# Two early flushes of postponed instructions, and keys moved before queries, in the routed-attention stage of a fused kernel

## The chip, the cores and the metric

The kernel runs on one core of one Trainium2 chip. The core has TensorE (PE; its weight loads are shown as PEld), VectorE (DVE), ScalarE (ACT), GpSimd (POOL) and SyncE (SP, which here only issues DMAs). The metric is device time in microseconds. Three timed runs of the kernel before took 784.69, 784.79 and 788.32 us, median 784.79.

## The reference

Three layers follow each other; all numbers are float32.

```
# 1: attention over pooled queries: B=4, H=8, S=1152, D=64
q_pool = q.reshape(B, H, 576, 2, D).mean(axis=3)
attn = softmax(q_pool @ k.T / 8);  y = attn @ v          -> x [4, 576, 512]
# 2: four causal attention experts; each token uses its best two
logits = x @ w_gate;  w = softmax over the two largest
for e in range(4):
    a = softmax(causal(x @ wq[e] @ (x @ wk[e]).T / 8))
    out += where(e chosen) * w * (a @ (x @ wv[e]) @ wo[e])
# 3: gated layer: causal convolution of 5 taps over the sequence
gate = sigmoid(conv(out));  result = (gate * (out @ w_val)) @ w_out
```

## The kernel before

Every engine's program is in the order in which the Python code calls the instructions; waits between engines are put in by the framework. Most float32 operands of a matmul are split in a high and a low half, and a product is the sum of three (high·high, low·high, high·low). So what TensorE makes in PSUM is evacuated twice: ScalarE writes the high half, VectorE the low one, which is the PSUM value less the high half (`split2`, L224 and L225).

The change lies in the second layer (stage 2, about 513 to 712 us of the span). For each batch b of four, experts go in two pairs g, and each pair has five query tiles in the order 1, 3, 2, 4, 0 (`ORDER`). That makes 40 steps n, ten for a batch: n = 10 to 14 are the first pair of b = 1, n = 20 to 24 that of b = 2. So n = 12 and n = 22 are the third tile (tile 2) of the first pair.

In step n the loop does the following, in this order: the normalisation factors of tile n - 1 (`norm2`, VectorE, then a multiplication on GpSimd, L786), the scores of tile n (`scores2`, L750 or L757 on TensorE; then maximum with the mask L759 and row minimum L760 on VectorE), one piece of filling work, the transposes of tile n - 2 (`transp2`, L822 or L810, evacuated in turn by ScalarE and VectorE, L798 and L800), the exponential of tile n (`expo2`, L771 or L773), and then more filling work up to a budget.

The filling work is the list `fill`. Its pieces are the projections of a pair (`proj`: for queries, w = 0, and keys, w = 1, two halves of 12 matmuls each, L242), the value projections (`vgate`, L275), the value products (`av2`, L837 and L850, which give y of a pair) and the output mix (`mix`, eight halves of six matmuls, L869, evacuated by L870 and L871). The mix of batch b - 1 is put on `fill` when y of its second pair is done; that falls in steps 12, 13 and 14 of the ten.

What a piece leaves for later goes on the list `late2`: the low half that VectorE makes (L225), the moves of a finished key or query tile (`move`: DMAs on SyncE from `hl` to the tiles that the scores read, four for keys, L256, and six for queries, L258 to L261), the four loads of a later batch's x (`load2`, L196), and, for `av2`, the function that puts the mix on `fill`. `late2` is emptied when the next piece has been issued (`pop`), or by `flush()`, which stands at the end of step 0 and of each tenth step, and at the start of a step when `fill` is empty. The conv taps of the mixed output (L215, VectorE) are `rides`: one or a few are issued behind a piece or at the end of a step.

PSUM for all the filling work is a pool of four buffers (`ps_m`); the tiles `hl` come from a pool of two.

Of the kernel before, what the change touches and what calls it, by code (L numbers as in the profile page):

```python
# [20 lines left out]
def tile_kernel(ctx, tc, q, k, v, w_gate, wq, wk, wv, wo, w_val, conv_w, w_out, wo_t, out):  # L21
# [42 lines left out]
    def f(ap):  # L64
        return ap.bitcast(F32)
# [127 lines left out]
    def load2(b):  # L193
        xh = xh_p.tile([P, KT, 2, SQ], F32R, name="xh")
        for t in range(KT):
            nc.sync.dma_start(f(xh[:, t]), f(x_d[b][:, t]))  # L196
        return [[xh[:, t, i] for i in range(2)] for t in range(KT)]
# [23 lines left out]
    late2, urgent, rides = [], [], []  # L221

    def split2(hi, lo, src, mul=1.0):
        act.activation(hi, src, AF.Copy, scale=mul)  # L224
        late2.append(lambda: dve.scalar_tensor_tensor(out=lo, in0=src, scalar=mul, in1=f(hi), op0=ALU.mult, op1=ALU.subtract))  # L225
# [3 lines left out]
    def proj(xh, g, then=None):  # L229

        box = {}

        def half(w, hf):
            if hf == 0:
                box[w] = hl2.tile([P, 2, SQ], F32R, name="hl")
            hl = box[w]
            cs = slice(w * ED + g * P, w * ED + (g + 1) * P)
            qsl = slice(hf * HQ, (hf + 1) * HQ)
            ps = ps_m.tile([P, 512], F32, name="a")
            ops = [(wi, xi, t) for t in range(KT) for wi, xi in THREE]  # L240
            for o, (wi, xi, t) in enumerate(ops):
                pe.matmul(ps[:, 0:HQ], lhsT=wqk[wi][:, t, cs], rhs=xh[t][xi][:, qsl], start=o == 0, stop=o == len(ops) - 1)  # L242
            split2(hl[:, 0, qsl], hl[:, 1, qsl], ps[:, 0:HQ], -scale if w == 0 else 1.0)
            if hf == 1:
                if w == 1 and then:
                    late2.append(then)
                late2.append(lambda: move(w))

        def move(w):
            hl = box[w]  # L250
            for r in range(2):
                rs = slice(64 * r, 64 * r + 64)
                for i in range(2):
                    src = hl[64 * i:64 * i + 64]
                    if w == 1:
                        nc.sync.dma_start(f(ks[g][i][rs]), f(src))  # L256
                    elif i == 0:
                        nc.sync.dma_start(f(qs[g][0][rs, 0:SQ]), f(src[:, r]))  # L258
                    else:
                        nc.sync.dma_start(f(qs[g][1][rs, 0:4 * P]), f(src[:, r, 0:4 * P]))  # L260
                        nc.sync.dma_start(f(qs[g][1][rs, SQ:]), f(src[:, r, 4 * P:]))  # L261

        return [(1.48, lambda w=w, hf=hf: half(w, hf)) for w in range(2) for hf in range(2)]

    def vgate(xh):
        v2 = v_p.tile([P, 5, ED + E], F32, name="v2")
# [442 lines left out]
    def value(yhs, b, m, hf, then):  # L709

        qsl = slice(hf * HQ, (hf + 1) * HQ)
        ps = ps_m.tile([P, 512], F32, name="a")
        ops = [(wi, yi, g) for g in range(EP) for wi, yi in THREE]
        for o, (wi, yi, g) in enumerate(ops):
            pe.matmul(ps[:, 0:HQ], lhsT=wf[:, g, wi, m * P:(m + 1) * P], rhs=yhs[b, g][:, yi, qsl], start=o == 0, stop=o == len(ops) - 1)  # L715
        late2.append(lambda: then(ps[:, 0:HQ], m, qsl))
# [16 lines left out]
    with ExitStack() as s2l:  # L733
# [61 lines left out]
        def evac(dst, src):  # L795
            turn[0] += 1
            if turn[0] % 2:
                act.activation(dst, src, AF.Copy)  # L798
            else:
                dve.tensor_copy(dst, src)  # L800
# [92 lines left out]
        def ahead(n):  # L893
            return (WORK[steps[n][2]][0] if n < len(steps) else 0) + (WORK[steps[n - LAG][2]][1] if LAG <= n < len(steps) + LAG else 0)
# [28 lines left out]
        def flush():  # L923
            now, late2[:] = late2[:], []
            for a in now:
                a()

        assert not fill and not late2 and not urgent
        for n in range(len(steps) + LAG):
            if n < len(steps):  # L930
                b, g, i = s = steps[n]
                if n % 5 == 0:
                    pts[b, g] = (pt_p2.tile([P, 4, 2, SQ], F32, name="pt"), pt_p2.tile([R64, 2, R64], F32, name="pt4"))
                    if g == 0 and b:
                        fill += proj(xh[b], 1, (lambda: xh.update({3: load2(3)})) if b == 2 else None)
                        if b == B - 1:
                            fill.append((0, lambda: late2.append(begin3)))
                    if n == 10 * B - 5:
                        buf = [f(c2.tile([P, 2, SQ], F32R, name=f"k20{i}")) for i in range(2)]
                        bufs = [c2.tile([P, SQ + R64], F32R, name=f"q20{i}") for i in range(2)]  # L940
                        v2 = v_p.tile([P, 5, ED + E], F32, name="v2").rearrange("p t c -> p (t c)")
                        first3["raw"] = [[buf[t // 2][:, t % 2] for t in range(KT)], [f(bufs[t])[:, 0:SQ] if t < 2 else v2[:, (t - 2) * SQ:(t - 1) * SQ] for t in range(KT)]]
                        raws = [(0.74, lambda i=i, m=m, hf=hf: value(yhs, i, m, hf, lambda ps, m, qsl: evac(first3["raw"][i][m][:, qsl], ps))) for i in range(2) for m in range(KT) for hf in range(2)]
                        fill += raws[0:14]
                    if b == 0 and g == 1:
                        buf = y0_p.tile([P, EP, 2, SQ], F32R, name="y0")
                        yhs.update({(0, i): buf[:, i] for i in range(EP)})
                    if b == 1 and g == 0:
                        buf = y12_p.tile([P, 2, EP, 2, SQ], F32R, name="y12")
                        yhs.update({(1 + j, i): buf[:, j, i] for j in range(2) for i in range(EP)})  # L950
                if n % 10 == 5 and b + 1 < B:
                    fill += proj(xh[b + 1], 0)
                if n % 10 == VG and b + 1 < B:
                    v2s[b + 1], gws[b + 1], vg = vgate(xh[b + 1])
                    fill += vg
                if n == 0:
                    fill += proj(xh[0], 1)
                if n == FD:
                    fill += [(2.6, lambda g=g: fold(g)) for g in range(EP)]
            t = 0.0  # L960
            left = 5 - n % 5
            own = [ahead(m) for m in range(n, n + left)]
            budget = max(FL, (sum(c for c, _ in fill) + (PEND if 10 <= n and n % 10 < PN else 0) + sum(own)) / left) - own[0]

            room = [3]

            def ride():
                if urgent:
                    urgent.pop(0)()
                    return  # L970
                if rides and room[0]:
                    room[0] -= 1
                    rides.pop(0)()

            def pop(rider=True):
                c, a = fill.pop(0)
                now, late2[:] = late2[:], []
                a()
                for x in now:
                    x()  # L980
                if rider:
                    ride()
                return c

            if 0 <= n - 1 < len(steps):
                norm2(steps[n - 1], gws[steps[n - 1][0]])
            if n < len(steps):
                scores2(s)
            if fill:
                t += pop(RD[n % 5])  # L990
            else:
                flush()
            if n >= LAG:
                b1, g1, i1 = steps[n - LAG]
                transp2(steps[n - LAG], pts[b1, g1])
                if i1 == ORDER[-1]:
                    if g1 == 1:
                        then = (lambda b1=b1: fill.extend(mix(b1, [yhs[b1, 0], yhs[b1, 1]]))) if b1 < B - 1 else begin_last
                    else:
                        then = (lambda: None) if b1 < B - 1 else load_wo3  # L1000
                    fill[IN:IN] = av2(v2s[b1], pts[b1, g1], g1, yhs[b1, g1], then)
            if n < len(steps):
                expo2(s)
            if n == 0:
                flush()
            while fill and t < budget:
                t += pop()
            ride()
            if n == 9:
                xh[2] = load2(2)  # L1010
            if n % 10 == 9:
                flush()
                while urgent:
                    urgent.pop(0)()
# [118 lines left out]
```

## Time and profile before

| | |
|---|---|
| timed runs, median | 784.79 us |
| profiled execution, its own time | 786.26 us |
| its span in the trace | 784.5 us |
| TensorE busy | 758.7 us (97%) |
| VectorE busy | 570.9 us (73%) |
| ScalarE busy | 448.4 us (57%) |
| GpSimd busy | 306.4 us (39%) |
| mean granted clock of TensorE | 0.998 |

The profiled execution is another one than the timed runs, and 1.47 us above their median. The span is what the trace holds; 1.76 us of the execution's time lie around it. The rows below name a line of the kernel, an engine, and what is written from what ("hl<-a" is the tile hl written from PSUM tile a). A figure in brackets is the time that the engine stood idle before the row, with what ended it.

### The profile page before, as it was taken

Reading aid. Unit: us, or ns where it says so; the run is one execution under the profiler, and the core shown is the slowest. Engines: PE = TensorE matmul, PEld = TensorE weight load, DVE = VectorE, ACT = ScalarE, POOL = GpSimd, SP = SyncE. Lnnn points to the kernel's source line nnn. Section 1 sums busy time; section 2 is a strip of 40 time slices with the busy share of each in tenths; the row PEclk is TensorE's granted clock in tenths of the full one; section 3 lists DMA queues with packets and bytes.
Section 4 is the critical chain, followed back from the end, with each engine's and each line's share of the span. In section 5 each row is a group of like instructions: output and inputs, shape, how many; then the busy total and the mean of one; then the engine's idle time right before and its main releaser. Section 6 shows DMA issues by size and latency. Waiting matters only on the chain.

```text
span 784.5 us, 14786 instructions
## 1 busy us (share of the span) xinstructions
PE 758.7 (97%) x5332; PEld 623.6 (79%) x5332; DVE 570.9 (73%) x1063; ACT 448.4 (57%) x988; POOL 306.4 (39%) x412
## 2 busy tenths in 40 slices
PE   6999999999999999999999999999989889989998
PEld 4777877878778778778778778898989779877887
DVE  5777888898988888567657756257679779887730
ACT  5665566566466566656656665344454554648532
POOL 4565575674765764652542501023222312230000
PEclk9999999999999999999999999999999999999999
DMA  7787868868878788667657581484524743900112
GB/s 237 179 204 221 242 185 228 243 181 236 208 238 241 204 239 257 178 184 209 155 162 229 135 293 43 92 239 102 162 67 123 199 99 92 302 8 14 73 63 94
DMA packets 86825, 134.51 MB, mean 171 GB/s; under 512 B 21600, under 2 KB 58976, under 8 KB 86752
## 3 DMA queue, kind: packets, MB, share of 16 engines
q1 hardware_dynamic: 86752, 133.57, 60.4%
q8 instruction: 42, 0.69, 0.4%
q14 instruction: 31, 0.25, 0.1%
HBM read 53.37 MB, written 21.76 MB: 96 GB/s over the span
## 4 chain that ended last, share of the span: by engine, by line
PE 84%; DVE 7%; DMA 3%; ACT 2%; SPq 1%; issue 1%; POOLq 0%; DVEq 0%; ACTq 0%
PE s L416 21%; PE t L464 19%; PE t L494 18%; PE o L1049 6%; PE a L242 5%; PE a L275 4%; DMA k<-hl 3%; PE a L850 2%; PE s L750 2%; PE a L715 2%; PE a L822 1%; DVE nm L760 1%; PE t L453 1%; PE a L869 1%; DVE gp L215 1%
## 5 line engine op out<-in xcount | busy, mean ns | idle before, releaser
L421 DVE TENSOR_REDUCE nm<-s 128x1 f32<-128x1152 f32 x144 | 195.5, 1358 | 37.0 <-PE s L416 30.9
L427 ACT ACTIVATE p<-s,nm 128x1152 f32<-128x1152 f32 x144 | 175.9, 1222 | 37.1 <-DVE nm L421 28.3
L464 PE MATMUL t<-ident,p 128*128 128x128 f32 x1296 | 194.1, 280 | 2.5 <-DVE pt L474 1.9
L472 ACT ACTIVATE pt<-t 128x384 f32<-128x384 f32 x224 | 99.9, 489 | 145.7 <-PE t L464 136.6
L464 PEld LDWEIGHTS t<-ident,p 128*128 128x128 f32 x1296 | 147.4, 141 | 41.1 <-ACT pt L472 17.0
L494 PE MATMUL t<-pt,vn 128*64 128x320 f32 (+1 forms) x1152 | 146.8, 409 | 0.0
L416 PE MATMUL s<-ka,qst 128*128 128x384 f32 x480 | 127.5, 369 | 6.8 <-ACT ka L545 6.8
L494 PEld LDWEIGHTS t<-pt,vn 128*64 128x64 f32 x1152 | 80.0, 137 | 55.8 <-issue 5.3
L416 PE MATMUL s<-kb,qst 128*128 128x384 f32 x480 | 121.1, 361 | 1.0 <-ACT p L427 0.9
L474 DVE COPY pt<-t 128x384 f32<-128x384 f32 x208 | 107.4, 548 | 13.1 <-PE t L464 9.6
L786 POOL TENSOR_TENSOR p<-p,sm 128x512 f32<-128x512 f32 (+3 forms) x32 | 40.1, 1253 | 122.1 <-DVE sm L784 96.3
L416 PEld LDWEIGHTS s<-kb,qst 128*128 128x128 f32 x480 | 79.8, 191 | 8.3 <-issue 6.2
L416 PEld LDWEIGHTS s<-ka,qst 128*128 128x128 f32 x480 | 78.1, 193 | 8.1 <-ACT ka L545 7.2
L442 POOL COPY rm<-rs 128x256 f32<-128x256 f32 x31 | 12.4, 399 | 130.1 <-PE t L464 73.3
L496 DVE TENSOR_TENSOR xf<-t,rb 128x256 f32<-128x256 f32 (+1 forms) x32 | 14.6, 458 | 63.1 <-PE t L494 62.3
L371 POOL TENSOR_TENSOR hlk<-kt,hlk 128x384 fp32r<-128x384 f32 x45 | 45.3, 1006 | 1.0
L771 ACT ACTIVATE p<-s,nm 128x256 f32<-128x256 f32 (+3 forms) x64 | 33.1, 525 | 19.4 <-DVE nm L760 19.4
L242 PE MATMUL a<-xh,wqk 128*128 128x288 f32 x288 | 42.7, 299 | 0.0
L503 POOL CAST xt<-xf 128x256 fp32r<-128x256 f32 (+1 forms) x32 | 13.6, 424 | 71.8 <-DVE xf L496 71.7
L215 DVE SCALAR_TENSOR_TENSOR gp<-x,cw,gp 128x572 f32<-128x572 f32 (+3 forms) x48 | 39.5, 825 | 0.5
L242 PEld LDWEIGHTS a<-xh,wqk 128*128 128x128 f32 x288 | 39.4, 188 | 0.4
L760 DVE TENSOR_REDUCE nm<-s 128x2 f32<-128x512 f32 (+4 forms) x40 | 32.4, 811 | 1.4
(176 smaller groups left out, 1095.5 us busy)
## 6 DMA issues: line engine op xcount, KB each, us to landing
ka<-hlk SPq DMA_DIRECT2D x90, 192.0 KB, 3.2
kb<-hlk SPq DMA_DIRECT2D x90, 192.0 KB, 3.6
vn<-in_v_dram SPq DMA_DIRECT2D x16, 576.0 KB, 7.6
k<-hl SPq DMA_DIRECT2D x32, 288.0 KB, 4.9
qt<-in_q_dram SPq DMA_DIRECT2D x15, 576.0 KB, 5.4
kt<-in_k_dram SPq DMA_DIRECT2D x15, 576.0 KB, 6.3
xh<-x_d SPq DMA_DIRECT2D x12, 576.0 KB, 6.5
x_d<-xt SPq DMA_DIRECT2D x16, 320.0 KB, 4.1
```

Source lines behind the costliest of these rows:

```text
L215: dve.scalar_tensor_tensor(out=gp[:, n:], in0=x[:, 0:SQ - n], scalar=cw[:, m, c:c + 1], in1=gp[:, n:], op0=ALU.mult, op1=ALU.add)
L242: pe.matmul(ps[:, 0:HQ], lhsT=wqk[wi][:, t, cs], rhs=xh[t][xi][:, qsl], start=o == 0, stop=o == len(ops) - 1)
L371: late.append(lambda: pool.tensor_tensor(out=hlk[:, 1, gs], in0=kt[:, gs], in1=f(hlk[:, 0, gs]), op=ALU.subtract))
L416: pe.matmul(ps[:, 0:GW], lhsT=a, rhs=c, start=o == 0, stop=o == len(ops) - 1)
L421: dve.tensor_reduce(d["nm"], d["s"][:, :, 0:GW], axis=AX.XY, op=ALU.min)
L427: act.activation(d["p"], d["s"][:, :, 0:GW], AF.Exp, bias=d["nm"], scale=-1.0, accum_out=sums[(2 * n + u) % len(sums)][:, i:i + 1])
L464: pe.transpose(ps[:, j * P:(j + 1) * P], p[:, g, j * P:(j + 1) * P], ident)
L472: act.activation(dst, src, AF.Copy)
L474: dve.tensor_copy(dst, src)
L494: pe.matmul(ps[64 * h:64 * h + 64, 0:N], lhsT=vn[:, h, j, :], rhs=pt[:, j, h, :], start=j == 0, stop=j == C - 1)
L760: dve.tensor_reduce(nm, ps[:, :, 0:w], axis=AX.X, op=ALU.min)
L1049: pe.matmul(ps[:, 0:w], lhsT=hl[xi][:, kt, t * P - a:(t + 1) * P - a], rhs=end3["wo3"][:, kt, wi, c:c + w], start=o == 0, stop=o == len(op ...
```

## The change

Two edits. At the end of steps 12 and 22 `flush()` is called. In `proj` the keys (w = 1) are projected and moved first, then the queries (w = 0); the loads of the next x (`then`, in batch 2 alone), which stood ahead of the key moves at the end of the projections, stand behind the query moves.

```
-                if w == 1 and then:
+                late2.append(lambda: move(w))
+                if w == 0 and then:
                     late2.append(then)
-                late2.append(lambda: move(w))
...
-        return [(1.48, lambda w=w, hf=hf: half(w, hf)) for w in range(2) for hf in range(2)]
+        return [(1.48, lambda w=w, hf=hf: half(w, hf)) for w in (1, 0) for hf in range(2)]
...
             if n == 9:
                 xh[2] = load2(2)
+            if n in (12, 22):
+                flush()
             if n % 10 == 9:
                 flush()
```

VectorE at the end of step 12 and the start of step 13; `y_6724` is y of the batch, `sm` the normalisation factors, `s` the scores and `nm` their minimum:

```order
 L225 SCALAR_TENSOR_TENSOR hl<-a,hl 128x288
-L780 TENSOR_SCALAR sm<-sm 128x2
-L781 RECIPROCAL sm<-sm 128x2
-L784 TENSOR_TENSOR sm<-sm,gw 128x2
-L759 TENSOR_TENSOR s<-s,cmask_78 128x64
-L760 TENSOR_REDUCE nm<-s 128x2
-L762 TENSOR_TENSOR nm<-nm 128x1
 L225 SCALAR_TENSOR_TENSOR y_6724<-a,y_6724 128x128
 L225 SCALAR_TENSOR_TENSOR y_6724<-a,y_6724 128x448
+L780 TENSOR_SCALAR sm<-sm 128x2
+L781 RECIPROCAL sm<-sm 128x2
+L784 TENSOR_TENSOR sm<-sm,gw 128x2
```

The two low halves of y now stand ahead of the factors of step 12 and the maximum and minima of step 13, which follow in the same order as before. Further on in steps 13 and 14, three conv taps stand behind the copy of the first transposes and ahead of the factors of the next tile, where none stood.

TensorE in step 13, from the second half of its scores on; `a<-y,wos` is the mix, `a<-ident,p` a transpose:

```order
 L757 MATMUL s<-k_6218,q_6214 128x288 x2
 L757 MATMUL s<-k_6219,q_6215 128x288 x2
+L869 MATMUL a<-y_6724,wos_95 128x288
+L869 MATMUL a<-y_6724,wos_96 128x288
+L869 MATMUL a<-y_6724,wos_95 128x288 x2
+L869 MATMUL a<-y_6724,wos_96 128x288
+L869 MATMUL a<-y_6724,wos_95 128x288
 L822 MATMUL a<-ident,p 128x128 x8
 L869 MATMUL a<-y_6724,wos_95 128x288
```

The first half of the mix moves ahead of the eight transposes. Four halves now stand ahead of the scores of step 14, where two stood; four follow them instead of six.

SyncE at the end of the projections of batch 2 (steps 20 to 22); `k_6220`, `k_6221`, `q_6216` and `q_6217` are the key and query tiles of the second pair, `xh` is x of batch 3, `g_d` the stored convolution. Before:

```order
L258 DMA q_6216<-hl 64x576
L260 DMA q_6217<-hl 64x512
L261 DMA q_6217<-hl 64x64
L880 DMA g_d_71<-gp 128x576
L196 DMA xh<-x_d_70 128x1152 x4
L256 DMA k_6220<-hl 64x1152
L256 DMA k_6221<-hl 64x1152
L256 DMA k_6220<-hl 64x1152
L256 DMA k_6221<-hl 64x1152
```

And now:

```order
L256 DMA k_6220<-hl 64x1152
L256 DMA k_6221<-hl 64x1152
L256 DMA k_6220<-hl 64x1152
L256 DMA k_6221<-hl 64x1152
L258 DMA q_6216<-hl 64x576
L260 DMA q_6217<-hl 64x512
L261 DMA q_6217<-hl 64x64
L258 DMA q_6216<-hl 64x576
L260 DMA q_6217<-hl 64x512
L261 DMA q_6217<-hl 64x64
L196 DMA xh<-x_d_70 128x1152 x4
```

The four key moves go from behind the loads to the front, and the loads stand behind all ten moves.

## Rows read from the trace of the kernel before

**Rows 1.** Waits of TensorE, 490 to 712 us: total, times, longest

```profile
PE a L869 <- DVE y L225: 2.6, 2, 1.3
PE s L750 <- issue: 1.7, 1, 1.7
PE a L869 <- ACT pt L798: 1.4, 2, 0.7
PE s L750 <- DMA k<-hl: 0.7, 2, 0.5
```

**Rows 2.** Timeline of TensorE, third batch, then second: start, us, instructions, idle before

```profile
614.25 0.44 PE L837 MATMUL a<-pt,v 128*64 128x128 f32 x4 [0.55 <-DVE pt L800]
618.80 1.04 PE L822 MATMUL a<-ident,p 128*128 128x128 f32 x8
631.53 0.47 PE L750 MATMUL s<-k,q 128*128 128x256 f32 x2 [1.70 <-issue]
632.58 1.76 PE L242 MATMUL a<-xh,wqk 128*128 128x288 f32 x12
...
564.22 0.44 PE L837 MATMUL a<-pt,v 128*64 128x128 f32 x4
581.67 1.76 PE L242 MATMUL a<-xh,wqk 128*128 128x288 f32 x12
```

**Rows 3.** Stretches after the mix waits, second and third batch: busy, PEclk, DMA, GB/s

```profile
572.00:578.00 6.00, 5.26 (x29) 5.26 (x30) 4.29 (x12) 3.66 (x10) 1.15 (x1) 0.72 0.20 40
620.00:626.00 6.00, 4.16 (x31) 3.92 (x32) 5.32 (x16) 3.66 (x10) 2.61 (x2) 1.00 1.03 342
```

**Rows 4.** Timeline of ScalarE and VectorE, steps 22 and 23

```profile
617.37 0.55 ACT L224 ACTIVATE y<-a 128x448 fp32r<-128x448 f32 x1 [1.85 <-PE a L850]
619.77 0.17 DVE L780 TENSOR_SCALAR sm<-sm 128x2 f32<-128x2 f32 x1 [2.35 <-ACT p L771]
621.91 0.81 DVE L225 SCALAR_TENSOR_TENSOR y<-a,y 128x128 fp32r<-128x128 f32 x2
```

**Rows 5.** Timeline, the operations of the chain in front of step 25

```profile
621.30 0.68 DVE L762 TENSOR_TENSOR nm<-nm 128x1 f32<-128x1 f32 x1
622.08 0.74 ACT L773 ACTIVATE p<-s,nm 128x576 f32<-128x576 f32 x1 [1.60 <-DVE nm L762]
625.93 0.55 DVE L800 COPY pt<-a 128x384 f32<-128x384 f32 x1
626.39 1.66 DVE L215 SCALAR_TENSOR_TENSOR gp<-x,cw,gp 128x573 f32<-128x573 f32 x2
626.98 0.44 ACT L870 ACTIVATE x<-a 128x288 f32<-128x288 f32 x1
627.27 0.54 ACT L871 ACTIVATE gp<-a,cw 128x288 f32<-128x288 f32 x1
...
601.08 0.15 DVE L780 TENSOR_SCALAR sm<-sm 128x1 f32<-128x1 f32 x1
602.28 0.42 DVE L760 TENSOR_REDUCE nm<-s 128x2 f32<-128x256 f32 x1
```

**Rows 6.** Timeline, a tap beside a GpSimd multiplication

```profile
642.39 1.89 POOL L786 TENSOR_TENSOR p<-p,sm 128x1024 f32<-128x1024 f32 x1 [4.12 <-DVE sm L784]
643.84 1.06 DVE L215 SCALAR_TENSOR_TENSOR gp<-x,cw,gp 128x575 f32<-128x575 f32 x1
```

**Rows 7.** SyncE's queue in step 22, and landing times, 600 to 640

```profile
616.38 2.07 SPq L196 DMA_DIRECT2D xh<-x_d  x4
618.54 2.67 SPq L256 DMA_DIRECT2D k<-hl  x4
...
k<-hl SPq DMA_DIRECT2D x4, 288.0 KB, 11.3
...
DMA to landing us min/median/max: 4.7/6.5/10.5
```

**Rows 8.** Stretch of steps 15 to 19: busy time of each engine

```profile
582.00:610.00 28.00, 28.00 (x218) 25.89 (x217) 25.76 (x65) 13.02 (x41) 6.16 (x5) 1.00 0.38 96
```

## The prediction

> **What bounds the kernel now.** I read the page's busy shares first: TensorE works for 97% of the span, so only time in which TensorE stands still, or runs slowly, can be won. The change touches the second stage alone, so the next view is the list of waits of TensorE in that stage [rows 1]. Four of its rows matter. Twice the output mix (L869) waits for the low half of y that VectorE makes (2.6 us together), twice just before that for ScalarE's copy out of PSUM (1.4), once the scores (L750) wait 1.7 us with no releaser named, and twice they wait for the key move (0.7 together, the longer 0.5). The timeline of TensorE gives the places [rows 2]. In the third batch (b = 2, step 22 and on) the value products (L837) start at 614.25. The mix waits fall in step 23 and the 1.70 in front of step 25, and the first projection of step 25 (L242) starts at 632.58: 18.33 us for this piece. The same piece of the second batch goes from 564.22 to 581.67, 17.45 us. Its TensorE work is the same, and it has the mix waits (2.0) but not the wait for keys (1.7 and 0.2). So by its waits the second batch should take 18.33 - 1.9 = 16.4. The missing 1.05 us is the clock: the granted clock is 0.72 of full over 572 to 578, so the lower of its two levels, 1.2 GHz, held for part of it after these waits, and 1.00 over 620 to 626 after the same waits of the third batch [rows 3].
>
> **The change part by part.**
>
> *The flush at the end of steps 12 and 22.* What it releases is the two low halves of y and the eight halves of the mix. Now VectorE makes y low at 621.91, behind the sums, maximum and minimum of the next tile, though ScalarE had y high at 617.92 and VectorE stood idle for 2.35 us until 619.77 [rows 4]. By the new order y low stands ahead of that group, so its 0.81 us falls into the idle time and is over by 618.8, when TensorE finishes the scores of step 23. The first half of the mix now stands there in the order, ahead of the eight transposes, and its PSUM buffer is not the one that the copy of those transposes frees. So both mix waits go, 2.0 us in each batch.
>
> *What is late next.* The piece of the third batch holds 18.33 - 2.0 - 1.7 - 0.2 = 14.4 us of TensorE work, so the projection of step 25 could start at 614.25 + 14.4 = 628.65. By the new order it must wait for a VectorE copy (L800, of the transposes of step 24), and ahead of that copy stand, since the mix comes out earlier, four conv taps instead of one. I follow VectorE from the end of L762 at 621.98, which nothing earlier moves [rows 5]. ScalarE then does the exponential of step 23 (0.74, and about 0.2 for its sum) and evacuates the second mix half (L870 and L871, 0.83 from start to end): the first tap can start at 623.75. VectorE then does three taps (0.83 each, 2.5), the six small operations from L780 to L760 (601.08 to 602.70, 1.62), a tap (0.8) and the copy (0.55), 5.45 in all. That is 629.2, a new wait of about 0.55 us in each of the two batches. Its bounds are nothing (the chain hidden) and 1.3 (each of these eleven operations 0.07 us longer than its row).
>
> One of the taps may be longer than its row. A tap beside a GpSimd multiplication took 1.06 us where one alone takes 0.80, and it ended 0.62 after that multiplication did [rows 6]; in the new order the fourth tap runs beside the multiplication of step 23. The Trainium skill (SBUF — State Buffer, section "SBUF: two separate sides") says that VectorE with two SBUF inputs and a GpSimd operation that reads SBUF take a shared port pair as an exclusive lock, the later one blocking until the first is done. The row agrees for the part that was blocked. By that rule each place loses 0.26 more and the gain is 0.5 less; the sum below goes without it, and the bound of 1.3 holds it.
>
> *Keys first, then queries.* No work is added: the projections, their evacuations and all the moves are the same. What is last is another transfer. The wait in front of step 25 (1.70 and 0.2) is for key moves that were issued at 618.54, behind the four loads of the next batch's x, and took 11.3 us in the median to land beside them [rows 7]. Now all ten moves stand in front of the loads. The keys go where the queries went, ahead of 616.38, and would need over 11 us from there to be late at 628; the queries, next, carry half their bytes. The wait goes: 1.9 us. The other key wait of [rows 1], the 0.5 at step 5, goes for the same reason.
>
> The loads pay for it. SyncE issues the same instructions between the same points, so the loads end where the key moves ended, at 618.54 + 2.67 = 621.2, instead of at 618.45. Loads landed 4.7 to 10.5 us after issue, 6.5 in the median [rows 7]: 627.7, or 631.7 at the longest. The first projection of step 25 needs its fourth load 1.2 us after it starts, at 630.4. In the median that is hidden; at the longest it costs 1.3 us once.
>
> *Sum.* Second batch: 17.45 - (629.2 - 614.25 = 14.95) = 2.5, of which 1.05 is the clock. Third batch: 18.33 - 14.95 = 3.4. Step 5: 0.5. Together 6.4. I take off 0.3 for the steps that follow, where VectorE runs about 1 us later against TensorE than now: 6.1. The profiled execution took 786.26, so by it 780.2. But the median of the three timed runs is 784.79, lower by 1.47, and a fall of the clock of about 1.05 in the profiled one alone would explain most of that. If the timed runs had no such fall, the gain is 5.0 and the time 779.8; if they had it, 784.79 - 6.1 = 778.7. The first is the nearer explanation. I take **779.6 us**.
>
> **The rivals.**
>
> *VectorE becomes the bound (17%).* In 582 to 610 VectorE works 25.76 of 28.00 us [rows 8], so it has 2.24 idle, and it is asked to come 2.5 earlier. If it can't, TensorE waits in steps 15 to 19 until it has given back the 2.5 of the second batch: 782.1. For it: the new wait above is already VectorE's. Against: the new order has two more taps (1.6 us) done before step 15 than the old one, so VectorE needs to find less than its idle time.
>
> *The chain is hidden (13%).* If the two new waits do not show, the gain is 7.5 by the profiled execution and 6.4 without the clock: 778.4.
>
> *The clock falls at a new place (10%).* The same two waits brought the lower level in one batch and not in the other [rows 3], and the new wait in front of steps 15 and 25 is shorter than either pair. If it falls once, 1.05 us: 780.7. The Trainium skill (TensorE: Matmul & The Clock Gate, Part 1) says that the block which watches TensorE's activity runs freely, so that the same kernel shows other cold stretches from run to run. By that rule, which these two batches bear out, the fall is chance and the timed median may well be without it, which is how I read the 1.47.
>
> *The loads of x become the bound, and it is slower (5%).* One mechanism, at step 25: the four loads now start behind ten moves and TensorE waits for the last of them. The gains elsewhere (2.5 + 0.5 - 0.3 = 2.7) and the place of the fourth load's matmuls in the old run (632.58 + 1.2 = 633.8) give the point at which everything is lost: a landing at 636.5, 15.3 us after the last issue. From there each us is one us lost; at 19.2 us the kernel takes 788.7. Against it: the longest landing seen is 10.5, beside moves that now have gone ahead.
>
> *It doesn't do what it says (3%).* Were the flush to find nothing to release, or the keys not last, the time would stay at 784.8. The order shows both moved, so little is left for this.
>
> **How the numbers follow.** My own forecast has 52%, with a range of its own of 778.4 to 781.3 (from 778.7 with nothing given back in the following steps, to 779.8 with both new waits at their bound, 0.75 more each). A measurement of this kernel tells about 0.5% from no change, that is 3.9 us: faster means below 780.9, slower above 788.7. Faster: 47 of my 52, the hidden chain's 13, 6 of the clock's 10, together 66%. Within 0.5%: 5 of mine, the 17 of VectorE, 4 of the clock's, 2 of the last, together 28%. Slower: the 5 of the loads and 1 for what I have not seen, 6%. The range for 8 times in 10 reaches from 777.4 (no new wait, and the clock's fall in the timed runs gone) to 783.2 (VectorE's case and somewhat more).
>
> **What would show it.** Right: the waits of the mix on VectorE's y and on ScalarE's copy are gone in both batches, y low starts within 1 us of y high, and no TensorE wait for a key or query move is over 0.2 us. The piece from L837 to L242 takes 14.4 to 15.7 us in both batches, with a wait for a VectorE copy in front of L242. Wrong: that wait is over 1.3 us, or waits for VectorE copies appear in front of L837 in steps 17 and 27, or L242 of step 25 waits for loads of x in its first 12 matmuls. A clock below 1.00 between 550 and 640 would put the clock's case in place of mine.

## The result and the profile after

In six timed runs of each, the kernel before took 785.92 us in the median and the changed kernel 779.27 (779.19 to 781.45); the ratio is 0.9912 [0.9894, 0.993], so the changed kernel is faster by 0.9%, and the interval lies below 1. The profiled execution took 779.28 us against 786.26, its span is 777.5 us against 784.5, and TensorE's granted clock was 1.0 against 0.998. 779.6 had been forecast.

Waits of TensorE in the second stage after the change (480 to 720 us; total, times, longest), beside [rows 1]:

```profile
PE a L242 <- DVE pt L800: 2.1, 2, 1.1
PE a L837 <- DVE pt L800: 1.4, 2, 0.8
...
PE s L750 <- DMA q<-hl: 0.2, 1, 0.2
```

The mix waits and both key waits are gone. A wait of 1.1 for the copy L800 in front of the projections has come twice, as forecast but twice the size. Of the waits in front of L837 two are left. The kernel before had four, in a row of the same view that [rows 1] leave out:

```profile
PE a L837 <- DVE pt L800: 2.5, 4, 0.8
```

The two that went had not been forecast.

Timeline of TensorE after, the rows that answer to [rows 2] (start, duration, instructions, idle before):

```profile
563.99 0.44 PE L837 MATMUL a<-pt,v 128*64 128x128 f32 x4
578.96 1.87 PE L242 MATMUL a<-xh,wqk 128*128 128x288 f32 x12 [1.07 <-DVE pt L800]
611.02 0.44 PE L837 MATMUL a<-pt,v 128*64 128x128 f32 x4
616.37 1.03 PE L822 MATMUL a<-ident,p 128*128 128x128 f32 x8
617.16 2.63 PE L869 MATMUL a<-y,wos 128*128 128x288 f32 x18
624.30 0.63 PE L750 MATMUL s<-k,q 128*128 128x256 f32 x4
626.00 1.99 PE L242 MATMUL a<-xh,wqk 128*128 128x288 f32 x12 [1.06 <-DVE pt L800]
```

The piece from L837 to L242 is 14.97 us in the second batch and 14.98 in the third, where it was 17.45 and 18.33; 14.95 had been forecast. The mix runs through behind the transposes, and the scores of step 25 wait for nothing. L837 of step 22 (611.02) has lost the 0.55 of idle time that [rows 2] show in front of it.

Busy time of PE, PEld, DVE, ACT and POOL, then PEclk, DMA share and GB/s of the changed kernel, for [rows 3] and [rows 8]:

```profile
572.00:578.00 6.00, 5.76 (x44) 5.31 (x42) 4.73 (x11) 4.27 (x14) 1.15 (x1) 1.00 0.05 9
620.00:626.00 6.00, 4.81 (x36) 4.37 (x36) 5.37 (x12) 4.27 (x15) 1.15 (x1) 1.00 1.00 368
582.00:610.00 28.00, 28.00 (x218) 25.88 (x217) 26.28 (x68) 12.76 (x41) 7.20 (x6) 1.00 0.39 96
```

The clock no longer falls in the second batch. In 582 to 610 TensorE never stands still in either kernel. VectorE does 26.28 us of work in it instead of 25.76; the changed kernel is some 3 us further on by then, so the stretch doesn't hold quite the same pieces.

VectorE and ScalarE in steps 22 to 24 of the changed kernel, for [rows 4 to 6]:

```profile
614.14 0.54 ACT L224 ACTIVATE y<-a 128x448 fp32r<-128x448 f32 x1 [2.34 <-PE a L850]
614.72 0.63 DVE L225 SCALAR_TENSOR_TENSOR y<-a,y 128x448 fp32r<-128x448 f32 x1 [0.82 <-ACT y L224]
616.54 0.17 DVE L780 TENSOR_SCALAR sm<-sm 128x2 f32<-128x2 f32 x1 [1.20 <-ACT p L771]
...
620.41 2.52 DVE L215 SCALAR_TENSOR_TENSOR gp<-x,cw,gp 128x572 f32<-128x572 f32 x3 [1.05 <-ACT gp L871]
623.72 1.15 POOL L791 TENSOR_TENSOR p<-p,sm 128x576 f32<-128x576 f32 x1 [4.97 <-PE a L869]
624.39 1.09 DVE L215 SCALAR_TENSOR_TENSOR gp<-x,cw,gp 128x575 f32<-128x575 f32 x1
625.40 0.55 DVE L800 COPY pt<-a 128x384 f32<-128x384 f32 x1
```

The larger part of y low now starts 0.04 us after its y high has ended, in what was idle time. Three taps, the small operations and a fourth tap stand ahead of the copy, whose end releases L242 at 626.00. The fourth tap runs beside GpSimd's multiplication and takes 1.09 us.

SyncE after, for [rows 7], and the landing of the loads of x:

```profile
610.18 3.23 SPq L256 DMA_DIRECT2D k<-hl  x4
613.51 0.82 SPq L258 DMA_DIRECT2D q<-hl  x1
...
618.85 2.19 SPq L196 DMA_DIRECT2D xh<-x_d  x4
...
DMA to landing us min/median/max: 4.1/5.5/6.9
```

The key moves go out 0.84 us ahead of L837 of step 22, where they went out 4.29 behind it (618.54 and 614.25 in [rows 7] and [rows 2]). The last load is issued by 621.04, 10.0 us behind that L837; the forecast had 621.2 - 614.25 = 6.95.

**Where the 7.0 us of span went.** Steps 12, 17, 22, 27 and 32 all have an L837, and the times between them give an account that stage 1 does not disturb. The last column is the sum of the four.

| kernel | 12 to 17 | 17 to 22 | 22 to 27 | 27 to 32 | 12 to 32 |
|---|---|---|---|---|---|
| before | 26.30 | 23.73 | 27.17 | 23.74 | 100.94 |
| after | 23.93 | 23.10 | 24.07 | 23.11 | 94.21 |
| flush alone (e1) | 23.93 | 23.11 | 28.76 | 23.11 | 98.91 |
| keys first alone (e2) | 26.31 | 23.74 | 25.93 | 23.73 | 99.71 |
| queries first, loads last (e3) | 23.93 | 23.10 | 24.78 | 23.10 | 94.91 |
| loads before the query moves (e4) | 23.93 | 23.11 | 29.34 | 23.11 | 99.49 |
| five taps in step 14 (e5) | 22.57 | 23.11 | 24.40 | 23.11 | 93.19 |
| the same, again (e9) | 22.58 | 23.10 | 24.06 | 23.11 | 92.85 |
| no taps in step 13 (e6) | 22.57 | 23.73 | 25.44 | 23.72 | 95.46 |
| after, again (e7) | 23.89 | 23.11 | 24.04 | 23.11 | 94.15 |
| moves earlier (e8) | 22.58 | 23.11 | 24.30 | 23.10 | 93.09 |
| loads by GpSimd (e10) | 22.59 | 23.10 | 25.25 | 23.11 | 94.05 |

Before to after that is 2.37 + 0.63 + 3.10 + 0.63 = 6.73 us; 0.57 more comes at step 5 (from step 0 to L837 of step 12), and stage 1 ended 0.34 later in this execution: 6.96.

### The profile page after: what moved, and what is told of

The parts are those of the page before. It is cut to its first block, busy times and chain, and to the rows that moved or that the text cites. A ratio compares the mean times of both kernels' runs of the same rounds, so it can differ in the third digit from the quotient of the medians.

```text
span 777.5 us, 14803 instructions
## 1 busy us (share of the span) xinstructions
PE 756.8 (97%) x5332; PEld 621.9 (80%) x5332; DVE 571.9 (74%) x1063; ACT 447.9 (58%) x988; POOL 306.5 (39%) x412
## 4 chain that ended last, share of the span: by engine, by line
PE 86%; DVE 7%; ACT 3%; issue 1%; SPq 1%; DMA 1%; POOL 1%; POOLq 0%; DVEq 0%; ACTq 0%
PE s L416 21%; PE t L464 20%; PE t L494 18%; PE a L242 7%; PE o L1051 6%; PE a L275 4%; PE a L850 3%; PE s L750 2%; PE a L715 2%; DVE gp L215 2%; PE a L822 1%; PE t L453 1%; SPq L524 1%; ACT p L771 1%; DVE nm L760 1%
## 5 line engine op out<-in xcount | busy, mean ns | idle before, releaser
L242 PE MATMUL a<-xh,wqk 128*128 128x288 f32 x288 | 43.0, 299 | 2.1 <-DVE pt L800 2.1
L242 PEld LDWEIGHTS a<-xh,wqk 128*128 128x128 f32 x288 | 39.4, 188 | 3.1 <-DVE pt L800 2.5
```

## The experiments

The kernel before took 786.56 us in the median beside e1 to e4, 786.37 beside e5 to e7, 787.43 beside e8 and e9, and 787.21 beside e10. Stage 1, which the change doesn't touch, adds differences of its own to these times. The clock fell in it in the profiled e1, e2, e5 and e6 (0.98 over the first 100 us), and at a granted clock of 1.00 throughout, the first projection of stage 2 still started anywhere from 492.3 (e7) to 494.6 us (e3). So the readings below rest on the table above and on rows.

**e1: the flush alone.** Keys and queries as before.

```
+            if n in (12, 22):
+                flush()
```

> The two flushes alone, queries projected and moved first as before. Mine (two separate waits, the later one covers the earlier in batch 2): the waits of the mix on y and on the copy go in both batches. The piece from L837 of step 12 to L242 of step 15 takes 15.0 us as in the changed kernel, but the piece from L837 of step 22 to L242 of step 25 stays near 18.3, since the keys still land behind the loads of x; the scores of step 25 then wait some 4 us for the key move. Step 5 keeps its 0.5 us. Time about 782 us. Rival (the gains add up): the third batch's piece falls to about 17, by the 2.0 us of the mix waits less the 1.06 of the new wait.

Measured: 783.62 us, ratio 0.9964 [0.9948, 0.998]. TensorE and SyncE in it:

```profile
581.36 1.87 PE L242 MATMUL a<-xh,wqk 128*128 128x288 f32 x12 [1.07 <-DVE pt L800]
...
629.85 1.47 PE L750 MATMUL s<-k,q 128*128 128x256 f32 x4 [2.98 <-DMA k<-hl]
631.11 3.08 PE L242 MATMUL a<-xh,wqk 128*128 128x288 f32 x12
...
614.43 2.05 SPq L196 DMA_DIRECT2D xh<-x_d  x4
616.58 2.50 SPq L256 DMA_DIRECT2D k<-hl  x4
```

The second batch is that of the changed kernel. In the third the key wait has grown to 2.98: TensorE comes sooner, and the keys not by as much. They are issued 3.15 us after L837 (4.29 before), and the scores start 16.42 us after it, where they started 17.28 after it before: of the 2.0 us of the mix waits 0.86 is left. The piece from L837 to L242 takes 17.68 us, between the 18.3 expected and the rival's 17; some 0.8 of it is slow clock, since the four scores take 1.26 us to the next matmul where they take 0.47 at the full clock (e2). So the waits don't add up, but the later one covers the earlier only in part. The granted clock was 0.83 over 620 to 640, falling after this wait, and with that the flush alone is a loss in this batch of the profiled execution (28.76 against 27.17).

**e2: keys first alone.** The changed kernel without the two lines of e1.

> Keys first alone, without the two flushes. Mine: the mix waits stay (2.0 us in each batch), the scores of step 25 wait for no move, so the third batch's piece from L837 to L242 takes 16.4 us and the second's 16.4 without a fall of the clock or 17.4 with one; step 5's 0.5 us goes. Time 782.1 us. Rival (the flush brings all, the key moves would have been early enough anyway): 784.5 us.

Measured: 784.9 us, ratio 0.9983 [0.9968, 0.9998]. TensorE, first in the second batch, then in the third:

```profile
565.67 0.44 PE L837 MATMUL a<-pt,v 128*64 128x128 f32 x4
583.13 1.76 PE L242 MATMUL a<-xh,wqk 128*128 128x288 f32 x12
...
615.72 0.44 PE L837 MATMUL a<-pt,v 128*64 128x128 f32 x4 [0.55 <-DVE pt L800]
621.99 0.93 PE L869 MATMUL a<-y,wos 128*128 128x288 f32 x5 [0.69 <-ACT pt L798]
624.23 1.19 PE L869 MATMUL a<-y,wos 128*128 128x288 f32 x7 [1.31 <-DVE y L225]
631.60 1.55 PE L242 MATMUL a<-xh,wqk 128*128 128x288 f32 x9
633.90 0.67 PE L242 MATMUL a<-xh,wqk 128*128 128x288 f32 x3 [0.74 <-DMA xh<-x_d]
```

The key wait is gone and the piece of the third batch is 15.88 us. With its two mix waits (0.69 and 1.31) taken off, TensorE's own work in the piece is 13.88 us. 0.74 of the gain is then waited for at the loads of x, which stand last. The waits in front of L837 stay: they belong to the flush, not to the order of keys and queries. The time lies near the rival's 784.5 and not at the 782.1 expected, but the rival's reason fails: the order alone takes the key wait away, and loses part of the gain again at the loads of x (25.93 in the table where it was 27.17).

**e3: the queries first as before, the loads behind the key moves,** and the flush.

```
-                if w == 1 and then:
-                    late2.append(then)
                 late2.append(lambda: move(w))
+                if w == 1 and then:
+                    late2.append(then)
```

> The two flushes and queries first as before, but the four loads of x stand behind the key moves. Mine (what made the keys late is the loads ahead of them, not that keys are last): no wait over 0.2 us for the keys at step 25, the pieces take 15.0 us, and only step 5 keeps its 0.5: 779.7 us. Rival (keys last are late since they carry twice the bytes): a wait of 1 to 2 us for the key move at step 25, 781 us.

Measured: 782.05 us, ratio 0.9943 [0.992, 0.9967].

```profile
628.19 1.46 PE L242 MATMUL a<-xh,wqk 128*128 128x288 f32 x9 [1.06 <-DVE pt L800]
630.25 0.66 PE L242 MATMUL a<-xh,wqk 128*128 128x288 f32 x3 [0.60 <-DMA xh<-x_d]
...
615.92 3.28 SPq L256 DMA_DIRECT2D k<-hl  x4
619.30 3.20 SPq L196 DMA_DIRECT2D xh<-x_d  x4
```

The keys are moved last, 2.70 us after L837 of step 22 where it was 3.15 in e1, and TensorE doesn't wait for them. So it was the four loads ahead of them that made them late. Being last costs something else: the loads come 0.60 late. The 779.7 expected was missed: this profiled execution took 2.9 us more than that of the changed kernel, 0.70 of it by the table, 0.57 by the key wait at step 5, which stays, and 1.64 in stage 1.

**e4: keys first, but the loads ahead of the query moves,** and the flush.

```
+                if w == 0 and then:
+                    late2.append(then)
                 late2.append(lambda: move(w))
-                if w == 0 and then:
-                    late2.append(then)
```

> The changed kernel, but the four loads of x stand behind the key moves and ahead of the six query moves. Mine (whatever stands behind the loads is late): the scores of step 25 wait for a query move, about 2 us, 781.3 us. Rival (the queries carry half the bytes and are hidden anyway): no wait over 0.2 us there, 779.3 us.

Measured: 783.55 us, ratio 0.9953 [0.9932, 0.9974].

```profile
627.57 1.20 PE L750 MATMUL s<-k,q 128*128 128x256 f32 x4 [3.74 <-DMA q<-hl]
```

In these runs whatever stands behind the loads is late, keys (e1) or queries. The size was missed: the wait is 3.74 where 2 had been expected, and the clock fell after it (0.83 over 620 to 640), so that 29.34 holds both.

**e5 and e9: taps behind the copy.** The number of conv taps allowed per step, 3 before, on top of the change.

```
-            room = [3]
+            room = [0 if n in (13, 23) else 5 if n in (14, 24) else 3]
```

> The changed kernel with one number altered: in steps 13 and 23 no conv tap is put behind VectorE's evacuations, in steps 14 and 24 five may be instead of three, so three taps move from ahead of the copy (L800) of step 14 and 24 to behind it. My theory (the wait of 1.07 us in front of L242 in steps 15 and 25 is VectorE's queue of taps ahead of that copy, and the 0.55 us waits in front of L837 in steps 22 and 32 went because taps were done earlier): both L242 waits fall to 0.2 or less, the pieces from L837 to L242 go from 14.97 to 13.9 to 14.1, the L837 waits of steps 22 and 32 stay away, and the time is about 2.1 us below the changed kernel in the same call, near 777.2. Rival (VectorE is the bound between steps 15 and 22 and must give back what it is asked to do sooner): the L242 waits go but waits of the same sum come back in front of L837 or the scores further on, and the time is that of the changed kernel, 779.3.

> The kernel with five taps in steps 14 and 24 once more, as the control for the one beside it: 93.2 us from L837 of step 12 to L837 of step 32, with a wait of about 1.25 us for x inside the first projection of step 25; 778 us where the clock does not fall.

Measured: 779.05 us, 0.9909 [0.9895, 0.9922]; again, 777.61 us, 0.9884 [0.9863, 0.9904]. TensorE in e5, first the second batch, then the third:

```profile
579.43 1.76 PE L242 MATMUL a<-xh,wqk 128*128 128x288 f32 x12
...
625.11 0.97 PE L242 MATMUL a<-xh,wqk 128*128 128x288 f32 x6
626.56 0.66 PE L242 MATMUL a<-xh,wqk 128*128 128x288 f32 x3 [0.49 <-DMA xh<-x_d]
627.98 0.67 PE L242 MATMUL a<-xh,wqk 128*128 128x288 f32 x3 [0.76 <-DMA xh<-x_d]
```

The waits for the copy are gone, both pieces are 13.76, and the waits in front of L837 stay away: the new wait was VectorE's queue of taps. VectorE gave nothing back in steps 15 to 22, so that rival falls. But only the second batch keeps the gain (23.93 to 22.57). In the third, TensorE reaches x a microsecond sooner and waits 1.25 (0.78 in e9) for loads that come when they came: 24.40 and 24.06 against 24.07. Beside the second batch, which waits for no x, that is 1.83 and 1.48 us, more than the gaps show. 2.1 had been expected, about 1.1 came.

**e6: no taps in steps 13 and 23,** steps 14 and 24 left at three.

```
-            room = [3]
+            room = [0 if n in (13, 23) else 3]
```

> The changed kernel with no conv tap behind VectorE's evacuations in steps 13 and 23, and the other steps unaltered: fewer taps are done by step 15 than in the changed kernel. My theory: the L242 waits of steps 15 and 25 go as well (1.07 and 1.06), but the taps are then as late as in the kernel before, so the 0.55 us waits in front of L837 of steps 22 and 32 come back: about 778.2, 1 us above the kernel that has five taps in steps 14 and 24. Rival (those L837 waits went for another reason, the order of the evacuations of keys and queries): none comes back and the two kernels agree within 0.3 us.

Measured: 781.24 us, 0.9935 [0.9922, 0.9947].

```profile
610.78 0.44 PE L837 MATMUL a<-pt,v 128*64 128x128 f32 x4 [0.55 <-DVE pt L800]
...
659.94 0.44 PE L837 MATMUL a<-pt,v 128*64 128x128 f32 x4 [0.54 <-DVE pt L800]
```

Both waits are back, 0.55 and 0.54. Two taps of 0.81 now run at 605.46 and 607.15, among VectorE's evacuations of steps 20 and 21, as in the kernel before (608.93 and 610.62); in the changed kernel the last tap of that batch ends by 602.0. So they had gone because taps are done earlier. That this kernel lies 2.2 above e5, where 1 was expected, is these two and 1.04 in step 25, where x comes 2.30 late (1.25 in e5). With the taps late, the store of the convolution (L880) stands on SyncE between the key and the query moves, at 613.71, ahead of the loads; in e5 it went out at 602.94.

**e7: the changed kernel again,** beside e5 and e6.

> The changed kernel itself, as the control for the two beside it on this chip. Every theory expects about 779.3 us where its clock does not fall, pieces from L837 to L242 of 14.97 in both batches with waits of 1.07 and 1.06 for L800 in front of L242.

Measured: 780.03 us (778.50 to 781.46), 0.9921 [0.9905, 0.9937]; the pieces from L837 to L242 and the waits in front of L242 are the same within 0.02.

**e8: the moves earlier.** On top of e5, to win back the wait for x:

```
-            if n in (12, 22):
+            if n in (12, 21, 22):
                 flush()
```

> The kernel with five taps in steps 14 and 24 (e5_taps_to_14), with one flush more, at the end of step 21: VectorE's evacuation of the last low half of the queries then stands ahead of the factors, sums and minima of step 22 instead of behind them (there it started at 613.78 us, though ScalarE had made its high half by 612.2), and with it the query moves and the loads of x behind them on SyncE go out about 1.5 us sooner. My theory (the 1.25 us that TensorE waits for x inside the first projection of step 25 are set by the place of the loads behind all ten moves): loads issued near 617.9 by that trace's time instead of 619.40, the wait for x down to 0.3 or less, the stretch from L837 of step 12 to L837 of step 32 from 93.2 to about 92.1 us, and 1 us less than e5_taps_to_14 in runs without a fall of the clock: near 777.0. Rival (the loads are set by the bandwidth or by their own latency behind the moves): they land at the same time, the wait stays over 0.9 and the stretch at 93.2. Second rival: the factors of step 22 are 0.5 us later, and TensorE waits in step 23 for what hangs on them.

Measured: 778.63 us, 0.9893 [0.9871, 0.9916]. SyncE in e8, then in e9, which is without this line:

```profile
608.60 3.28 SPq L256 DMA_DIRECT2D k<-hl  x4
617.27 2.12 SPq L196 DMA_DIRECT2D xh<-x_d  x4
```

```profile
608.50 3.27 SPq L256 DMA_DIRECT2D k<-hl  x4
616.53 2.19 SPq L196 DMA_DIRECT2D xh<-x_d  x4
```

A miss: the loads go out no sooner. I had read the start of the query moves as set by VectorE's low half; the low half now starts 0.83 us after L837 (2.42 in e9), but the first query move still starts 2.72 after it, as in e9, because the key moves hold SyncE until then (3.28 us for four). The ten moves stand back to back for 8.6 us (7.9 in e9). The wait for x was 1.14 here and 0.78 in e9, without the edit.

**e10: the loads by GpSimd's queue,** on top of e5.

```
-                        fill += proj(xh[b], 1, (lambda: xh.update({3: load2(3)})) if b == 2 else None)
+                        fill += proj(xh[b], 1, (lambda: xh.update({3: load2(3, nc.gpsimd)})) if b == 2 else None)
```

> The kernel with five taps in steps 14 and 24 (e5_taps_to_14), with the four loads of x of batch 3 issued by GpSimd's queue, behind its multiplication of step 22, instead of by SyncE's behind the ten moves. The last experiment left the loads' issue where it was, 7.4 to 8.0 us after L837 of step 22, since the ten moves stand back to back on SyncE for 8.6 us from the key move on. Theory (SyncE's issue of the ten moves sets when the loads start): they are issued about 3.3 us after L837, 4 us sooner, the wait for x in the first projection of step 25 (0.78 to 1.25 in the two runs without this) goes, no key or query wait over 0.3 comes in its place, and the stretch from L837 of step 12 to L837 of step 32 falls from 92.7 to 93.2 to about 92.0: 776.6 to 777.0 us without a fall of the clock. Rival (it is the transfers that share the 16 engines): the loads land sooner, but the scores of step 25 wait for queries by 1 to 3 us, as they did when the loads stood ahead of the query moves in one queue, and the time is 778 to 780.

Measured: 779.4 us, 0.991 [0.9887, 0.9934]. GpSimd, TensorE, and the landing of loads and moves in e10:

```profile
613.99 2.33 POOL L196 DMA_DIRECT2D xh<-x_d  x4
...
625.62 0.47 PE L750 MATMUL s<-k,q 128*128 128x256 f32 x2 [1.37 <-DMA q<-hl]
626.86 0.51 PE L750 MATMUL s<-k,q 128*128 128x256 f32 x2 [0.76 <-DMA q<-hl]
...
xh<-x_d POOLq DMA_DIRECT2D x4, 576.0 KB, 9.9
...
q<-hl SPq DMA_DIRECT2D x2, 128.0 KB, 9.2
```

The loads go out 3.2 us after L837 instead of 7.4, and x is no longer waited for. But the query moves now take 9.2 us to land instead of 4.5 in the changed kernel, and the scores wait 2.13 for them: the rival was right. A queue of their own doesn't help here; loads and moves share something on the way, and the mean busy share of the 16 DMA engines was 1.00 to 1.04 over 614 to 626.

The best version run is the changed kernel with five taps in steps 14 and 24 (e5, e9). Four of the six runs of e9 took 777.25 to 777.75 us, eight of the twelve of the changed kernel 778.50 to 779.69; side by side the medians are 779.05 and 780.03. The intervals of their ratios overlap, so that the gain of about 1 us rests on the table.

## Why the prediction was right, and where it was not

- **The mix waits go (2.0 in each batch): right.** The flush alone removes them (e1), keys first alone leaves them (e2).
- **The place of the new wait: right, its size not.** L242 was forecast 14.95 us after L837 and came after 14.97 and 14.98. But the wait itself is 1.06, not 0.55, because the step "18.33 - 2.0 - 1.7 - 0.2 = 14.4 us of TensorE work" was wrong: e2 shows 13.88. The key wait had cost 18.33 - 2.0 - 13.88 = 2.45 us, not 1.9. Besides the two gaps shown, the second pair of scores was pulled apart from the first by 0.3: from the first score to L242 1.05 us passed in the kernel before and 0.47 in e2, and the gap shown in it is 0.26. The 0.5 too little in the wait taken away and the 0.5 too little in the new one cancel, since the sum used the end of VectorE's chain.
- **The clock: right in kind, too small.** By the same 13.88 the fall in the second batch cost 17.45 - 2.0 - 13.88 = 1.57 us, not 1.05. e2, which keeps the waits, shows it directly: 17.46 in the second batch, with a granted clock of 0.91 over 560 to 580, and 15.88 in the third, with no fall after the same waits.
- **The clock in the timed runs: not borne out.** The prediction called this fall chance and took the three timed runs to be without it. The Trainium skill (TensorE: Matmul & The Clock Gate, Part 1) says of the slow stretch at a kernel's start that it differs from run to run of one kernel. The mean granted clocks of the timed runs do differ from run to run (1.00 in 8 of the 12 runs of the changed kernel, 0.997 to 0.998 in the others). But the two traces that hold the mix waits in both batches, of the kernel before and of e2, have the fall in the same place. And the mean clock was below 1.00 in 54 of 59 runs of the kernel before beside the experiments and in all ten of e2, against 20 of 39 of the kernels with neither mix waits nor a wait for moves in step 25 (after, e3, e5 to e9). That is a hint that the fall comes with the waits in most runs, and no proof, since stage 1 has falls of its own. For the six runs of the kernel before beside the result no clock was recorded. Their times gain 6.65 us by the medians and 5.2 by the fastest runs (784.42 and 779.19), against 7.0 in the profiled pair.
- **The tap beside GpSimd.** It was blocked: 1.09 us against 0.80 alone, ending 0.61 after the multiplication's end at 624.87, as the Trainium skill (SBUF — State Buffer, section "SBUF: two separate sides") has it. So do all ten taps in the two traces, before and after, that start over 0.4 us ahead of such a multiplication's end: they end 0.61 or 0.62 after it. Yet the sum without that 0.26 came out, by luck, since the rest of the chain was shorter by as much: the first tap starts 9.39 us after L837 (9.50 forecast), and from there to the fourth tap 3.98 us pass (4.12 forecast).
- **Keys first: right, and the reason was the right one.** The keys were late because they stood behind the loads (e3, e4), not because they were last. Step 5: 0.57 measured, 0.5 forecast.
- **The loads of x hidden: right, but by less than forecast.** Against L837 they are issued 3 us later than the step had it, which took over a time of the old run although the ten moves hold SyncE for 8.6 us from the first key move on. Landing was quicker in return, 4.1 to 6.9 us (4.7 to 10.5 in [rows 7]), with no moves beside them. Nothing waits for them in the changed kernel, but the cover is the new wait: without it they are late by 0.78 to 1.25 in the gaps shown and by 1.5 to 1.8 in the table (e9, e5).
- **"0.3 for the steps that follow": incomplete.** Behind the pieces 0.11 and 0.25 were given back, close to that. What I left out is the gain on the other side: with two more taps done before step 15, VectorE has none among its evacuations of steps 20 and 21, and the waits in front of L837 in steps 22 and 32 go, 0.63 each in the table. I had listed "two more taps done" only as a reason why VectorE would not lose. e6 puts them back, and the waits with them.

So the sum of 6.1 was, as measured, 0.57 + 2.48 + 3.35 + 1.26 - 0.36 = 7.3 in the profiled pair, and would be 7.3 - 1.57 = 5.7 where the clock does not fall. That the forecast came within 0.4 us of the median is partly luck. It took 5.2 off 784.79, the median of three runs; the measured gain is 6.65 from 785.92, the median of six. The gain was too small, above all by the 1.26 in front of L837 and 0.52 of the clock, and the time that it was taken from too low by 1.13. The rivals: VectorE as the bound is refuted by the changed kernel, which never stands still in 582 to 610, and by e5; the chain was not hidden; the clock fell nowhere in the second stage of the profiled execution; and the loads of x became late only with another edit.

Left open: why one and the same pair of mix waits brings the clock down in the second batch and not in the third, and what in the transfers (the engines, which were busy throughout in e10, or the memory at either end) loads and moves share; neither was tried.

## What to carry to other kernels

When a wait is taken out, list what becomes late next, with its time: here each gain met the next wait (copy, then x, then queries), and in the third batch e5 to e10 only moved the last microsecond from one wait to the other. Price a removed stall by the piece of work with and without it, not by adding up the gaps in the trace: the gaps understated it by 0.5 us for the keys, and by 0.6 to 0.7 for x in e5 and e9. And work that an engine does earlier is missing later; look there for a gain as well as for a loss.

## What the runs showed of the hardware

The key moves of the third batch landed in 11.3 us (before) and 11.7 us (e1) behind four loads of 576 KB each in their queue, and in 5.3 us without them (after, e3); with the loads in another queue the query moves of 128 KB landed in 9.2 us (e10) instead of 4.5 (after). Issuing ten moves in a row held SyncE for 7.9 us (e9, e10) to 8.6 us (after, e5, e8). A conv tap that started over 0.4 us ahead of the end of a GpSimd multiplication took 1.06 to 1.09 us where one alone took 0.80. After waits of 2.98 and 3.74 us in front of the scores (e1, e4) the granted clock was 0.83 over 620 to 640; after two waits of 0.7 and 1.3 it fell in the second batch only (0.91 over 560 to 580), and after waits of 1.37 and 0.76 (e10) and of 1.53 and 0.77 (e6) it stayed at 1.00.
